# A diffusion transformer block on one core: finer first loads, Q stepped over its rows, and modulation work moved to later stages

## Chip, cores, metric

The kernel runs on one core of one Trainium2 chip. The time is device time in microseconds (us) of one execution. Times of runs made in one session share that session's executions of the kernel before, and where I compare kernels of two sessions I compare their ratios to it.

## The reference, cut to what matters

B = 2 sequences of N = 256 tokens, D = 1152 features, H = 2 heads, F = 4608; everything in bf16.

```python
mod = (_silu(c) @ w_mod).reshape(B, 6, 1, D)
shift_a, scale_a, gate_a, shift_m, scale_m, gate_m = [mod[:, i] for i in range(6)]
h = _layernorm(x, axis=-1) * (1 + scale_a) + shift_a
qkv = (h @ wqkv).reshape(B, N, 3, H, Dh)
...                                          # softmax(q k^T) v, per head
a = ... @ wo
x = x + gate_a * a
h2 = _layernorm(x, axis=-1) * (1 + scale_m) + shift_m
m = _gelu(h2 @ w_fc1) @ w_fc2
return x + gate_m * m
```

So the stages on TensorE are: scale vector and K (which can start with scale_a alone; the shift is added later), Q, scores, V, attention times V, w_o, the first MLP matrix, the second. About 48 MB of weights are read once, roughly in that order. LN2 below is the second layer norm, that of h2; a "hole" is a stretch in which TensorE stands idle.

## The kernel before: the parts that matter

The token tiles are t = 0..3 (two per batch), the feature blocks k = 0..8. All loads go out in order on one queue.

```python
for b in range(B):                                   # x in two loads
    nc.sync.dma_start(x_sb[:, b * TPB:(b + 1) * TPB, :], x_v[:, b, :, :])
KGROUPS = [(0, 2), (2, 4), (4, 6), (6, 9)]           # scale columns and K rows, in turn
for k0, k1 in KGROUPS:
    nc.sync.dma_start(w_scale_a[:, :, k0 * P:k1 * P], ...)
    nc.sync.dma_start(w_k[:, k0:k1, 0:KM1 * P], ...)
nc.sync.dma_start(w_k[:, :, KM1 * P:D], ...)
w_shift_a = load_rows("w_shift_a", ...)
w_q = load_panels("w_q", wqkv_v, 0)                  # three column panels
w_gate_a, w_v, w_shift_m, w_scale_m, w_o, w_f1[0], w_f1[1] = ...   # load_rows each
...
warm(2, pwarm)                                       # matmuls on zeros, 512 columns
nc.tensor.transpose(pc[:], c_sb[:], ident[0:B * KD, 0:B * KD])
...
warm(14, pwarm)
act_stats()                                          # tile 1 on ScalarE, others on VectorE
for j in range(NPD):
    stats_piece(0, j)
...                                                  # tile by tile: norm, transpose, modulate, K
for m in range(KD):                                  # Q, one 128-column block at a time
    for k in range(KD): ...matmul(pacc, w_q[:, k, m * P:(m + 1) * P], hT[:, k, :])
    evac(qT[:, m, :], pacc[:], attn_scale)
    if m == 6:
        gate_a = gate_natural(0, w_gate_a)           # matmuls, then out to DRAM and back, broadcast
```

The w_o stage is pipelined in program order: the statistics of a group are emitted after the multiply of the next one. LN2's normalised rows go through a DMA transpose that ScalarE issues.

```python
BETWEEN = {2: ((0, "d"), (1, "d"), (2, "a"), (3, "a")), 3: ((8, "d"),)}
...
for o, (t, i) in enumerate(order):
    last = o == len(order) - 1
    if last:
        ln2_modulate(0, 4)
    wo_group(t, i, i < NPD - 1)                      # 9 matmuls, times gate_a, plus x
    if o:
        ln2_stats(*order[o - 1])                     # after a tile's third: sqrt, BETWEEN[t], norm,
    if last:                                         # and nc.scalar.dma_start_transpose
        ln2_modulate(0, 5, "a")                      # "a": on ScalarE
        ln2_modulate(0, 7, "a")
        ln2_modulate(0, 6)
```

Of the kernel before, what the change touches and what calls it, by code (L numbers as in the profile page):

```python
# [19 lines left out]
def kernel(  # L20
# [64 lines left out]
    for b in range(B):  # L85
        nc.sync.dma_start(x_sb[:, b * TPB:(b + 1) * TPB, :], x_v[:, b, :, :])
# [11 lines left out]
    KGROUPS = [(0, 2), (2, 4), (4, 6), (6, 9)]  # L98
# [3 lines left out]
    for k0, k1 in KGROUPS:  # L102
        nc.sync.dma_start(
            w_scale_a[:, :, k0 * P:k1 * P],
            wmod_v[:, :, S_SCALE_A * D + k0 * P:S_SCALE_A * D + k1 * P],
        )
        nc.sync.dma_start(w_k[:, k0:k1, 0:KM1 * P], wqkv_v[:, k0:k1, D:D + KM1 * P])
    nc.sync.dma_start(w_k[:, :, KM1 * P:D], wqkv_v[:, :, D + KM1 * P:2 * D])
# [10 lines left out]
    def load_panels(name, view, col0):  # L119
        w = wide_tile(name)  # L120
        for n in range(NPD):
            nc.sync.dma_start(w[:, :, n * PW:(n + 1) * PW], view[:, :, col0 + n * PW:col0 + (n + 1) * PW])
        return w

    w_shift_a = load_rows("w_shift_a", wmod_v, S_SHIFT_A * D)
    w_q = load_panels("w_q", wqkv_v, 0)
    w_gate_a = load_rows("w_gate_a", wmod_v, S_GATE_A * D)
    w_v = load_rows("w_v", wqkv_v, 2 * D)
    w_shift_m = load_rows("w_shift_m", wmod_v, S_SHIFT_M * D)
    w_scale_m = load_rows("w_scale_m", wmod_v, S_SCALE_M * D)  # L130
    w_o = load_rows("w_o", wo_v, 0)
    w_f1 = [None] * 4
    w_f1[0] = load_rows("w_f1_0", wfc1_v, 0)
    w_f1[1] = load_rows("w_f1_1", wfc1_v, D)
# [23 lines left out]
    warm(2, pwarm)  # L158
# [9 lines left out]
    nb1 = small.tile([P, NT], FP32, name="nb1", tag="nb1", bufs=1)  # L168
# [9 lines left out]
    T_ACT = 1  # L178
# [5 lines left out]
    def act_stats():  # L184
        for f, dst in ((ACT.Identity, dsum), (ACT.Square, dsq)):
            nc.scalar.activation(
                xns[T_ACT][:], x_sb[:, T_ACT, :], f, bias=pivot, scale=-1.0, accum_out=dst[:],
            )
# [15 lines left out]
    def recip1(t, with_nb=False):  # L204
        nc.vector.reciprocal(rstd1[:, t:t + 1], rstd1[:, t:t + 1])
        if with_nb:
            nc.vector.scalar_tensor_tensor(
                nb1[:, t:t + 1], mv1[:, t, 0:1], -1.0, rstd1[:, t:t + 1], op0=ALU.mult, op1=ALU.mult
            )

    def norm1(t, c0, c1, eng):
        if eng == "a":
            nc.scalar.activation(
                xns[t][:, c0:c1], x_sb[:, t, c0:c1], ACT.Identity,
                bias=nb1[:, t:t + 1], scale=rstd1[:, t:t + 1],
            )
        else:
            nc.vector.tensor_scalar(
                xns[t][:, c0:c1], x_sb[:, t, c0:c1], mv1[:, t, 0:1], rstd1[:, t:t + 1],
                op0=ALU.subtract, op1=ALU.mult,  # L220
            )
# [4 lines left out]
    def scale_group(g):  # L226
        k0, k1 = KGROUPS[g]
        pm = aux_tile([P, k1 - k0, B], "pm")
        for j in range(k0, k1):
            for k in range(KD):  # L230
                nc.tensor.matmul(
                    pm[:, j - k0, :], w_scale_a[:, k, j * P:(j + 1) * P], sT[:, k, 0:B],
                    start=(k == 0), stop=(k == KD - 1),
                )
        return lambda: nc.vector.tensor_scalar_add(scale_a[:, k0:k1, :], pm[:], 1.0)
# [8 lines left out]
    def modulate(pt, i, k, t0, j0, w, eng):  # L244
        b = t0 // TPB
        dst, src, sc = hT0[:, k, t0 * P:t0 * P + w], pt[:, i, j0:j0 + w], scale_a[:, k, b:b + 1]
        if eng == "d":
            nc.vector.tensor_scalar_mul(dst, src, sc)
        else:
            nc.scalar.mul(dst, src, sc)  # L250

    def modulated_transpose(k):
        pt = transpose_x([k], range(NT))
        for b in range(B):
            modulate(pt, 0, k, b * TPB, b * N, N, "da"[k % 2])
# [41 lines left out]
    CUT = 4 * P  # L297
    warm(14, pwarm)
    act_stats()
    for j in range(NPD):  # L300
        stats_piece(0, j)
    stats_piece(2, 0)
    stats_piece(2, 1)
    add0 = scale_group(0)
    sqrt1(0)
    act_stats_finish()
    recip1(0, True)
    sqrt1(T_ACT)
    norm1(0, 0, CUT, "d")
    add0()  # L310
    pt_0 = transpose_x([0, 1], [0])
    recip1(1)
    modulate(pt_0, 0, 0, 0, 0, P, "a")
    modulate(pt_0, 1, 1, 0, 0, P, "a")
    norm1(1, 0, CUT, "d")
    warm(2, pwarm)
    pt_1 = transpose_x([0, 1], [1])
    modulate(pt_1, 0, 0, 1, 0, P, "a")
    modulate(pt_1, 1, 1, 1, 0, P, "a")
    k_step(0, 0, P)  # L320
    k_step(1, 0, P)
    stats_piece(2, 2)
    sqrt1(2)
    for j in range(NPD):
        stats_piece(3, j)
    k_step(0, P, N)
    norm1(0, CUT, D, "a")
    sqrt1(3)
    recip1(2)
    warm(1, aux_tile([P, T], "pwarm2"))  # L330
    pt_2 = transpose_x([2, 3], [0, 1])
    scale_group(1)()
    k_step(1, P, N)
    modulate(pt_2, 0, 2, 0, 0, N, "a")
    modulate(pt_2, 1, 3, 0, 0, N, "a")
    norm1(2, 0, CUT, "d")
    recip1(3)
    norm1(3, 0, CUT, "d")
    k_step(2, 0, N)
    for ks, e in (((0, 1), "d"), ((2, 3), "a")):  # L340
        pt_3 = transpose_x(ks, [2, 3])
        for i, k in enumerate(ks):
            modulate(pt_3, i, k, 2, 0, N, e)
    k_step(3, 0, N)
    norm1(1, CUT, D, "d")
    norm1(2, CUT, D, "d")
    norm1(3, CUT, D, "d")
    k_step(0, N, T)
    scale_group(2)()
    k_step(1, N, T)  # L350
    modulated_transpose(4)
    k_step(2, N, T)
    modulated_transpose(5)
    k_step(3, N, T)
    k_step(4)
    scale_group(3)()
    modulated_transpose(6)
    k_step(5)
    modulated_transpose(7)
    k_step(6)  # L360
    modulated_transpose(8)
# [8 lines left out]
    def vec_section(stat, w, name):  # L370
        pn = aux_tile([P, CTW], "pn")
        for k in range(KD):
            wk4 = w[:, k, :].rearrange("p (j q r) -> p q j r", q=4, r=32)
            for i in range(4):
                nc.tensor.matmul(  # L375
                    pn[32 * i:32 * i + SW, :].rearrange("p (j r) -> p j r", r=32),
                    stat[:, k, :], wk4[:, i, :, :],
                    start=(k == 0), stop=(k == KD - 1), tile_position=(0, 32 * i),
                )
        dst = act.tile([P, KD, 32], FP32, name=name)  # L380
        nc.vector.transpose(dst[:].rearrange("p k c -> p (k c)"), pn[:])
        return dst
# [5 lines left out]
    shift_a = vec_section(sT, w_shift_a, "shift_a")  # L388
    k_panel(8)

    hT = act.tile([P, KD, T], BF16, name="hT")
    for k in range(KD):
        for b in range(B):
            dst, src = hT[:, k, b * N:(b + 1) * N], hT0[:, k, b * N:(b + 1) * N]
            if (k * B + b) % 3 < 2:
                nc.vector.tensor_scalar_add(dst, src, shift_a[:, k, b:b + 1])
            else:
                nc.scalar.activation(dst, src, ACT.Identity, bias=shift_a[:, k, b:b + 1])
# [69 lines left out]
    gate_a = None  # L468
    for m in range(KD):
        pacc = acc_tile([P, T], "pacc")  # L470
        for k in range(KD):
            nc.tensor.matmul(  # L472
                pacc[:], w_q[:, k, m * P:(m + 1) * P], hT[:, k, :],
                start=(k == 0), stop=(k == KD - 1),
            )
        evac(qT[:, m, :], pacc[:], attn_scale)
        if m == 6:
            gate_a = gate_natural(0, w_gate_a)



# [11 lines left out]
    def attn_transpose(i):  # L493
        pair = attn_all[:, TPB * i:TPB * (i + 1), :].rearrange("p i n -> p (i n)")
        nc.scalar.dma_start_transpose(attnT_all[:, i, :].rearrange("p (c n) -> p c n", n=P), pair)
# [21 lines left out]
    def softmax(b, h):  # L517
# [10 lines left out]
        def finish():  # L528
# [6 lines left out]
            attn_transpose(i)  # L535
# [15 lines left out]
    for i, (pnl, t) in enumerate(v_order):  # L551
        if i < len(softmaxes):
            softmaxes[i]()
        v_group(pnl, t)
        if i == 9:
            shift_m = vec_section(sT, w_shift_m, "shift_m")
            scale_m = vec_section(sT, w_scale_m, "scale_m")
            nc.vector.tensor_scalar_add(scale_m[:, :, 0:B], scale_m[:, :, 0:B], 1.0)

    w_f1[2] = load_rows("w_f1_2", wfc1_v, 2 * D)  # L560
# [8 lines left out]
    def av_tile(chunks, b):  # L569
        pa = acc_tile([P, len(chunks), N], "pa")  # L570
        for ci, cc in enumerate(chunks):
            for kc in range(TPB):
                vt = v_sb[:, b * TPB + kc, cc * P:(cc + 1) * P]
                dst = pa[:, ci, :].rearrange("p (q n) -> p q n", n=P)
                for h in (range(H) if cc == HC else [cc // HC]):
                    rows = half(h) if cc == HC else slice(0, P)
                    av = nc.tensor.matmul(  # L577
# [4 lines left out]
        return av  # L582

    for b in range(B):
        for chunks in ((0, 1), (2, 3), (5, 6), (7, 8)):
            av = av_tile(chunks, b)
            if b == 0 and chunks[0] == 0:
                tc.add_manual_dep(first_load["w_f1_0"], av.ins.name, WAIT_FOR, reason="transposes first")
# [63 lines left out]
    for o, (t, i) in enumerate(order):  # L652
# [3 lines left out]
        wo_group(t, i, i < NPD - 1)  # L656
        if o:
            ln2_stats(*order[o - 1])
# [33 lines left out]
    for b in range(B):  # L692
# [13 lines left out]
        if b == 0:  # L706
            mods = [ln2_modulate(1, k) for k in range(KD)]
            tc.add_manual_dep(first_load["w_f1_2"], mods[0].ins.name, WAIT_FOR, reason="transposes first")
# [84 lines left out]
```

## Time and profile before

| | before |
|---|---|
| time, median | 245.31 us (245.11 to 245.61) |
| TensorE busy | 237.0 of 244.1 us |
| mean granted clock | 1.000 |
| first scale matmul / first K matmul | 9.13 / 10.70 us |
| first MLP matmul / last matmul begins | 98.76 / 240.07 us |

From the page of the kernel before: the span, TensorE's busy time (busy us, share, instructions), the granted clock in 40 slices in tenths, and the first line of the chain that ended last, by engine.

```profile
span 244.1 us, 3930 instructions
...
PE 237.0 (97%) x1679; PEld 142.6 (58%) x1679; DVE 91.7 (38%) x198; ACT 62.1 (25%) x122; POOL 25.4 (10%) x37
...
PEclk9999999999999999999999999999999999999999
...
PE 89%; DVE 4%; DMA 2%; ACT 2%; ACTq 1%; issue 1%; DVEq 0%
```

TensorE is all that counts. It is busy for almost the whole span, so an edit can only win time in which it waits or runs slowly. The granted clock of the page has its first record at 8.96 us here, when the clock went to full; the digits before it read 9 because nothing is on record there, and the spacing of the matmuls shows the half speed instead (warm-ups 0.427 us apart, 0.216 us later). The step to full is called the switch below.

The timeline of TensorE at the start (start us, length us, engine, line, operation, out<-in, shapes, count; in brackets the idle time before and who ended it):

```profile
3.35 5.95 PE L156 MATMUL pwarm<-zeros 128*128 128x512 bf16 x14
9.13 0.59 PE L231 MATMUL pm<-sT,w_scale_a 128*128 128x2 bf16 x18
...
9.70 0.59 PE L156 MATMUL pwarm<-zeros 128*128 128x512 bf16 x2
...
10.70 1.17 PE L263 MATMUL pk<-big,w_k 128*128 128x128 bf16 x18
...
13.53 0.82 PE L263 MATMUL pk<-big,w_k 128*128 128x256 bf16 x6 [0.44 <-ACT big L250]
```

Read it so: 14 warm-up matmuls of 512 columns take 5.95 us, 0.427 us each, twice what such a matmul takes later (0.216 us start to start). They last until the first scale weights are there (landed at 8.72 us in the trace). K then begins in pieces of 128 columns, and there are waits for normalised rows.

The same view at the first MLP matrix:

```profile
81.20 17.72 PE L632 MATMUL pacc<-w_o,big 128*128 128x384 bf16 x108
98.76 3.44 PE L682 MATMUL pacc<-hT,w_f 128*128 128x256 bf16 x30
102.55 65.14 PE L682 MATMUL pacc<-hT,w_f 128*128 128x256 bf16 x393 [0.36 <-ACT hT L600]
```

```profile
99.17 1.35 ACT L622 ACTIVATE xn<-x,nb,rstd 128x1152 bf16<-128x1152 f32 x1
100.55 1.30 ACTq L623 DMA_TRANSPOSE hT<-xn  x1
101.90 1.09 ACT L600 ACTIVATE hT<-hT,shift_m,scale_m 128x256 bf16<-128x256 bf16 x2 [1.38 <-issue]
```

After 30 matmuls TensorE stops for 0.36 us by the view; measured start to start (from one matmul's start to the next one's, less the usual spacing) it is 0.52 us. It waits for a modulation on ScalarE (line L600).

### The profile page before, as it was taken

How to read it: one execution, taken by the hardware profiler on the slowest of the kernel's cores; microseconds unless marked ns; L12 is line 12 of the kernel's file. 1: busy time of each engine (PE TensorE's matmuls, PEld its weight loads, DVE VectorE, ACT ScalarE, POOL GpSimd, SP SyncE). 2: the span in 40 equal slices, each digit the busy share in tenths (PEclk: the TensorE clock that was granted, in tenths of full speed). 3: DMA queues.
4: the chain of work that ended last, by engine and by line, in shares of the span. 5: the costliest groups of instructions: out<-in, count | busy, mean ns of one | idle time of the engine just before them, and what ended most of it. 6: DMA issues, size and time to landing. Idle time of an engine off the chain costs nothing.

```text
span 244.1 us, 3930 instructions
## 1 busy us (share of the span) xinstructions
PE 237.0 (97%) x1679; PEld 142.6 (58%) x1679; DVE 91.7 (38%) x198; ACT 62.1 (25%) x122; POOL 25.4 (10%) x37
## 2 busy tenths in 40 slices
PE   6999999999999999999999999999999999999993
PEld 2585444456667665788854444444665656565673
DVE  2761562126414589913006999910000000000001
ACT  6632251145122521671422233322000000000000
POOL 1000000031000233200000000001222111111111
PEclk9999999999999999999999999999999999999999
DMA  6999999999996999227999994799300000010000
GB/s 227 327 333 360 371 326 390 391 390 393 342 374 93 385 392 182 48 51 249 393 392 374 326 327 121 221 327 320 102 16 16 19 16 16 17 33 19 16 19 16
DMA packets 47308, 53.28 MB, mean 218 GB/s; under 512 B 8371, under 2 KB 34107, under 8 KB 47291
## 3 DMA queue, kind: packets, MB, share of 16 engines
q1 hardware_dynamic: 39840, 50.14, 61.0%
q10 hardware_dynamic: 6939, 1.71, 5.1%
q0 software_dynamic: 512, 1.19, 1.4%
q8 instruction: 13, 0.21, 0.4%
q14 instruction: 4, 0.03, 0.0%
HBM read 50.14 MB, written 1.19 MB: 210 GB/s over the span
## 4 chain that ended last, share of the span: by engine, by line
PE 89%; DVE 4%; DMA 2%; ACT 2%; ACTq 1%; issue 1%; DVEq 0%
PE pacc L738 29%; PE pacc L682 28%; PE pacc L543 7%; PE pacc L472 7%; PE pk L263 4%; PE pk L292 2%; PE pwarm L156 2%; PE pacc L632 2%; PE pa L577 2%; PE ps_s L501 2%; PE pn L375 1%; DMA hT<-xn 1%; DVE stats L646 1%; DMA c_sb<-in_c_dram 1%; DVE tmp L637 1%; ACT xn L622 1%
## 5 line engine op out<-in xcount | busy, mean ns | idle before, releaser
L682 PE MATMUL pacc<-hT,w_f 128*128 128x256 bf16 (+1 forms) x432 | 70.7, 326 | 0.4 <-ACT hT L600 0.4
L738 PE MATMUL pacc<-w_f,gT 128*128 128x384 bf16 (+2 forms) x468 | 70.5, 314 | 0.0
L738 PEld LDWEIGHTS <-gT 128*128 128x128 bf16 x468 | 44.4, 98 | 26.2
L682 PEld LDWEIGHTS <-w_f 128*128 128x128 bf16 x432 | 42.2, 98 | 28.2 <-issue 0.5
L744 DVE TENSOR_TENSOR tmp<-pacc,gate 128x384 f32<-128x384 f32 (+2 forms) x13 | 6.8, 526 | 65.6 <-PE pacc L738 57.8
L714 ACT ACTIVATE gT<-pacc 128x512 bf16<-128x512 f32 x24 | 14.3, 597 | 32.7 <-PE pacc L682 32.7
L424 DVE SCALAR_TENSOR_TENSOR part<-w_gate_m,s,part 128x1152 f32<-128x1152 bf16 x16 | 21.3, 1413 | 0.0
L543 PE MATMUL pacc<-w_v,hT 128*128 128x384 bf16 x108 | 17.9, 326 | 0.0
L472 PE MATMUL pacc<-hT,w_q 128*128 128x512 bf16 x81 | 17.8, 379 | 0.0
L632 PE MATMUL pacc<-w_o,big 128*128 128x384 bf16 x108 | 17.7, 326 | 0.0
L746 POOL TENSOR_TENSOR o_sb<-tmp,x 128x384 bf16<-128x384 f32 (+1 forms) x12 | 11.6, 970 | 54.4 <-DVE tmp L744 54.4
L632 PEld LDWEIGHTS <-big 128*128 128x128 bf16 x108 | 10.5, 98 | 7.0 <-issue 0.2
L543 PEld LDWEIGHTS <-hT 128*128 128x128 bf16 x108 | 10.4, 98 | 7.2 <-issue 0.4
L263 PE MATMUL pk<-big,w_k 128*128 128x256 bf16 (+2 forms) x90 | 13.4, 294 | 0.4 <-ACT big L250 0.4
L472 PEld LDWEIGHTS <-w_q 128*128 128x128 bf16 x81 | 7.8, 98 | 9.9 <-DMA w_q<-in_wqkv_dram 0.5
L638 POOL TENSOR_TENSOR x<-tmp,x_sb 128x384 f32<-128x384 f32 x8 | 7.3, 912 | 35.3 <-DVE tmp L637 35.3
L263 PEld LDWEIGHTS <-w_k 128*128 128x128 bf16 x90 | 7.5, 98 | 3.4 <-issue 0.4
L156 PE MATMUL pwarm<-zeros 128*128 128x512 bf16 x19 | 8.0, 580 | 1.2 <-DVE eps_t L93 1.2
L703 ACT ACTIVATE gT<-pacc 128x512 bf16<-128x512 f32 x12 | 6.5, 598 | 9.5 <-PE pacc L682 9.5
L422 DVE TENSOR_SCALAR part<-w_gate_m,s 128x1152 f32<-128x1152 bf16 x2 | 1.6, 818 | 17.6 <-DMA w_gate_m<-in_w_mod_dram 17.6
L446 POOL DMA_DIRECT2D gates_dram<-nat_v x2 | 1.1, 531 | 68.0 <-DVE nat_v L444 68.0
L637 DVE TENSOR_TENSOR tmp<-pacc,gate 128x384 f32<-128x384 f32 x12 | 6.6, 547 | 2.7 <-PE pacc L632 2.7
(93 smaller groups left out, 156.4 us busy)
## 6 DMA issues: line engine op xcount, KB each, us to landing
w_f<-in_w_fc_dram SPq DMA_DIRECT2D x14, 864.0 KB, 10.2
w_f<-in_w_fc_dram SPq DMA_DIRECT2D x2, 2592.0 KB, 15.5
w_f<-in_w_fc_dram SPq DMA_DIRECT2D x2, 1728.0 KB, 10.5
w_shift_a<-in_w_mod_dram SPq DMA_DIRECT2D x3, 864.0 KB, 11.4
w_q<-in_wqkv_dram SPq DMA_DIRECT2D x3, 864.0 KB, 12.0
w_gate_a<-in_w_mod_dram SPq DMA_DIRECT2D x3, 864.0 KB, 10.0
w_v<-in_wqkv_dram SPq DMA_DIRECT2D x3, 864.0 KB, 13.3
w_shift_m<-in_w_mod_dram SPq DMA_DIRECT2D x3, 864.0 KB, 15.2
```

What stands on the lines that cost most here:

```text
L156: nc.tensor.matmul(dst[:], zeros[:, 0:P], zeros[:], start=True, stop=True)
L263: nc.tensor.matmul(pk[m][:, c0:c1], w_k[:, k, m * P:(m + 1) * P], hT0[:, k, c0:c1], start=(k == 0 and c0 == 0), stop=(k == KD - 1), skip_g ...
L424: nc.vector.scalar_tensor_tensor(part[:, b, :], wg[:, k, :], s32[:, k, b:b + 1], part[:, b, :], op0=ALU.mult, op1=ALU.add,)
L472: nc.tensor.matmul(pacc[:], w_q[:, k, m * P:(m + 1) * P], hT[:, k, :], start=(k == 0), stop=(k == KD - 1),)
L543: nc.tensor.matmul(pacc[:], hT[:, k, t * P:(t + 1) * P], w_v[:, k, pnl * PW:(pnl + 1) * PW], start=(k == 0), stop=(k == KD - 1),)
L632: nc.tensor.matmul(pacc[:], aT[:, k, t * P:(t + 1) * P], w_o[:, k, c0:c1], start=(k == 0), stop=(k == KD - 1),)
L637: nc.vector.tensor_tensor(tmp[:], pacc[:], gate_a[:, b, c0:c1], op=ALU.mult)
L638: (nc.gpsimd if pool_add else nc.vector).tensor_tensor(x1[:, t, c0:c1], tmp[:], x_sb[:, t, c0:c1], op=ALU.add)
L682: nc.tensor.matmul(dst, w_f1[m // KD][:, k, ml * P:(ml + 1) * P], hT[:, k, c0:c1], start=start, stop=(k == KD - 1), **kw,)
L714: nc.scalar.activation(gT[:, m, :], pacc[:], ACT.Gelu_apprx_tanh)
L738: nc.tensor.matmul(pacc[:], gT[:, kk, t * P:(t + 1) * P], w_f2[j][:, r, c0 - n * PW:c0 - n * PW + cw], start=(kk == 0), stop=(kk == KF - 1),)
L746: (nc.vector if last else nc.gpsimd).tensor_tensor(o_sb[:], tmp[:], x1[:, t, c0:c0 + cw], op=ALU.add)
```

## The change

The intent, as far as the diff tells: let the first token tile arrive alone and start its statistics sooner, take the first matmuls in whole batches, keep loads just ahead of use (w_shift_a in two column groups between the rows of Q, Q stepped over k), bring w_o forward, and hold the modulation and MLP loads until the attention transposes are done. Three single warm-up matmuls that the kernel before has in the holes of the front (at 9.70, 9.91 and 11.70 us in its trace) are gone. The core of the diff, with cuts:

```diff
-    for b in range(B):
-        nc.sync.dma_start(x_sb[:, b * TPB:(b + 1) * TPB, :], x_v[:, b, :, :])
+    for t in range(TPB):
+        nc.sync.dma_start(x_sb[:, t, :], x_v[:, 0, t, :])
+    nc.sync.dma_start(x_sb[:, TPB:2 * TPB, :], x_v[:, 1, :, :])
...
-    KGROUPS = [(0, 2), (2, 4), (4, 6), (6, 9)]
+    SGROUPS = [(0, 2), (2, 4), (4, 6), (6, 8), (8, 9)]
...
-    w_q = load_panels("w_q", wqkv_v, 0)
+    SHG = [(0, 5), (5, 9)]
+    QROWS = [[(0, 3), (3, 5)], [(5, 7), (7, 9)]]
+    for (j0, j1), rows in zip(SHG, QROWS):           # shift columns, then rows of Q
...
+    w_v = load_rows("w_v", wqkv_v, 2 * D)
     w_gate_a = load_rows("w_gate_a", wmod_v, S_GATE_A * D)
-    w_v = load_rows("w_v", wqkv_v, 2 * D)
-    w_shift_m = ...
-    w_scale_m = ...
     w_o = load_rows("w_o", wo_v, 0)
...
-    warm(2, pwarm)
+    warm(4, pwarm)
...
-    warm(14, pwarm)
+    warm(13, pwarm)
...                                                  # statistics: tile 2 on ScalarE
+    norm1(0, 0, CUT, nc.vector)                      # CUT: 256 columns
+    norm1(0, CUT, D, nc.gpsimd)                      # the other 896 on GpSimd; the same for tile 1
...                                                  # K in steps of 256 columns
+    vec_section(sT, w_shift_a, shift_a, *SHG[0])
+    shift_chunks(*SHG[0])
...
+    for k in range(KD):                              # Q stepped over k, six accumulators
+        for m in range(KM1):
+            q_mm(m, k)
+        if k == 3:
+            vec_section(sT, w_shift_a, shift_a, *SHG[1])
+            shift_chunks(*SHG[1])
...                                                  # in V:
-        if i == 9:
-            shift_m = ...; scale_m = ...
+        if i == 7:
+            gate_a = gate_natural(0, w_gate_a)
...
+    tc.add_manual_dep(first_load["w_shift_m"], transposed.ins.name, WAIT_FOR, ...)
...                                                  # in w_o:
+        if o == 2:
+            vec_section(sT, w_shift_m, shift_m)
+        if o == 5:
+            vec_section(sT, w_scale_m, scale_m)
```

## The prediction

> **What bounds it now.** TensorE. The page gives PE 237.0 of 244.1 us (97%); the chain of waits is PE for 89%. From 13.5 us on the matmuls stand back to back (timeline: 128x512 every 0.216 us). Only time in which PE waits or warms up can be won. Timeline and chain show: 9.13 us before the first scale matmul (after warm-up matmuls; its weights landed at 8.72); then to 13.5 us about 1.7 us: three warm-up matmuls (0.64), waits for the normalised rows of token tile 1 (0.46) and for modulation on ACT (0.60); 0.15 at 19.9 us (last scale group, landed 20.19); 0.2 at 33.9 us (first Q panel, landed 34.08); 0.52 at 102 us (first MLP matmuls wait for LN2). Winnable after 9.13 us: about 2.6 us, 1%.
>
> **What the change does, costed.**
> 1. Token tile 0 lands alone: the first half of x landed at 4.83 us, so its statistics start about 0.7 us sooner. But scale group 0 has the same bytes ahead of it and still lands near 8.7, and 13 cold warm-up matmuls of 0.427 us still end near 8.9. [...] Four early warm-ups may bring the switch forward. Gain 0.2 to 0.4 us.
> 2. The chain statistics, sqrt, reciprocal, norm is re-cut. With the durations of before (statistics piece 0.47, aggregate 0.24, sqrt 0.29, norm 0.35 to 0.5) I schedule: scale group 0 at 8.95, K from 10.2 (before 10.7); idle 0.6 before it, 0.7 before the transposes of batch 1 (norms of tiles 2 and 3 done at 12.2), 0.7 before its second transposes (896-column norms, done at 15.2). Holes 2.0 us against 1.7: the front gives back what point 1 wins.
> 3. Scale groups of two blocks and Q by rows: the waits at 19.9 and 33.9 us vanish: -0.35.
> 4. shift_a in two sections. One section of 36 matmuls takes 1.29 us: four column groups side by side, 0.122 us for 288 columns, plus 0.1 at each change over. Two with 160 and 128 columns: estimated +0.2 to +0.6 us.
> 5. Q stepped over k in six accumulators: same matmuls, no new wait (evictions of 0.6 to 0.7 us on two engines fit).
> 6. gate_a in V and the modulation sections in the w_o stage: the same PE time, moved. The attention transposes run without competing loads (before, 9 to 14 us to landing), but PE did not wait for them. Token tiles 0 and 1 finish about 1.4 us sooner and the sections (2.3 us) cover LN2: -0.5 us at 102 us. gate_a lands near 82 us; six accumulators absorb it.
>
> **Net** about -0.5 us. Predicted 244.9 us, range 243.4 to 246.4. Faster by over 2%: 2%; within 2%: 95%; slower by over 2%: 3%.
>
> **What would show it.** Scale matmuls from 8.7 to 9.0 us, K at 10.2; PE idle 1.5 to 2.2 us in all between 9 and 16 us; no PE wait on the last scale group or on Q; two shift_a sections at 1.5 to 1.9 us together; attention transposes landing in about 4 us; no PE idle in the first MLP matmuls; PE end 0.3 to 1 us sooner.
>
> **What would make it wrong.** The clock warming much later or sooner; GpSimd's norm holding up VectorE; [...] gate_a so late that LN2 slips and the MLP waits; the held loads arriving late for the modulation sections or the MLP.

Two passages are cut from this text: in point 1 the reason that I gave for a switch that comes sooner, and one of the risks. With the middles of the ranges, -0.3 (point 1), +0.3 (the holes of point 2), -0.35, +0.4 and -0.5 us make -0.45, which I wrote as about -0.5. That four early warm-ups may bring the switch forward, and the 0.2 to 0.4 us for it, were my estimate: the trace of before shows the spacing of the warm-ups go from 0.427 to about 0.215 us at 8.9 us, and not what sets that moment. The norms of 0.35 to 0.5 us in point 2 are an estimate too: before has norms of 512 and 640 columns on VectorE, of 0.41 and 0.44 us, and the line through these gives 0.35 us for 256 columns and 0.50 for 896.

## The result

The changed kernel takes 249.34 us (248.86 to 249.64, 4 runs) against 245.31 us: ratio 1.0161, 95% interval 1.0144 to 1.0179. It is slower by 4.0 us, where I had expected it to be 0.4 us faster, and it lies outside my range. A ratio here is the mean time of one kernel's runs over that of the other's of the same rounds, so it is not quite the ratio of the medians.

The same lines of the page, after:

```profile
span 247.5 us, 3960 instructions
...
PE 237.6 (96%) x1685; PEld 142.7 (58%) x1695; DVE 92.7 (37%) x199; ACT 61.1 (25%) x118; POOL 32.2 (13%) x39
...
PEclk9959999999999999999999999999999999999999
...
PE 79%; DMA 9%; DVE 5%; ACT 2%; issue 1%; POOL 1%; ACTq 1%; SPq 0%; DVEq 0%; POOLq 0%
```

TensorE's busy time hardly moved, but the third of the forty slices shows a clock of 0.5, and only 79% of the chain is TensorE. The mean clock of the four executions was 0.985, 0.985, 0.986 and 0.992; none of the 40 executions of the kernel before whose clock is listed was under 0.996. The start of TensorE's timeline:

```profile
3.14 3.55 PE L161 MATMUL pwarm<-zeros 128*128 128x512 bf16 x13
9.10 0.60 PE L224 MATMUL pm<-sT,w_scale_a 128*128 128x2 bf16 x18 [2.41 <-DMA w_scale_a<-in_w_mod_dram]
...
10.42 2.04 PE L250 MATMUL pk<-big,w_k 128*128 128x256 bf16 x12 [0.47 <-DVE big L240]
12.93 0.61 PE L234 MATMUL pt<-ident,xn 128*128 128x128 bf16 x4 [0.46 <-DVE xn L211]
...
13.97 1.44 PE L250 MATMUL pk<-big,w_k 128*128 128x256 bf16 x6
...
17.53 1.70 PE L250 MATMUL pk<-big,w_k 128*128 128x256 bf16 x12
```

The thirteen warm-ups now take 3.55 us in place of 5.95. In the trace they are 0.216 us apart from the fourth on, at 4.4 us. They end at 6.5 us and TensorE stands idle until 9.1 us. Then the K matmuls of 256 columns, twelve in 2.04 us, change their spacing at 11.2 us from 0.109 to 0.213 us, and back at 18.0 us. The windows view, 11 to 18 us, before and then after (length, then busy us of each engine, granted clock, DMA share, GB/s):

```profile
11.00:18.00 7.00, 6.56 (x107) 6.01 (x105) 5.08 (x18) 3.37 (x9) 0.00 (x0) 1.00 1.11 332
```

```profile
11.00:18.00 7.00, 6.53 (x54) 4.58 (x52) 3.60 (x14) 1.53 (x4) 1.79 (x1) 0.51 1.16 320
```

In these 7 us TensorE looks as busy as before, 6.53 us, but at half the granted clock (0.51 for 1.00). It ran 54 matmuls in place of 107; since their shapes differ, count the columns that they streamed: about 6900 in place of 12900. In 3.42 us that end 0.1 us before the clock fell, it was busy for 1.50 us, less than half the time (same view of the kernel after):

```profile
7.65:11.07 3.42, 1.50 (x29) 1.31 (x29) 2.48 (x9) 2.48 (x6) 3.42 (x2) 1.00 1.12 342
```

The w_o stage and the first MLP matmuls, after:

```profile
92.53 8.95 PE L642 MATMUL pacc<-w_o,big 128*128 128x384 bf16 x54
102.10 3.43 PE L697 MATMUL pacc<-hT,w_f 128*128 128x256 bf16 x30 [0.62 <-DVE hT L613]
106.10 22.19 PE L697 MATMUL pacc<-hT,w_f 128*128 128x256 bf16 x193 [0.57 <-ACT hT L610]
```

There are 0.62 and 0.57 us of idle time where there was 0.36, and a wait that was not there before is at the head of this stage (list of waits, total us, times, longest):

```profile
DVE tmp L647 <- DMA gate<-gates_dram: 4.9, 1, 4.9
```

In the trace gate_a lands at 86.2 and 87.5 us; w_o's first group was done at 82.6. I had put the landing at 82 us. In the kernel before it landed at 62.7 and 65.2 us.

### The profile page after: what moved, and what is told of

Same layout as the page of the kernel before. It is cut to its first block, busy times and chain, and to the rows that moved or that the text cites. A ratio compares the mean times of both kernels' runs of the same rounds, so it can differ in the third digit from the quotient of the medians.

```text
span 247.5 us, 3960 instructions
## 1 busy us (share of the span) xinstructions
PE 237.6 (96%) x1685; PEld 142.7 (58%) x1695; DVE 92.7 (37%) x199; ACT 61.1 (25%) x118; POOL 32.2 (13%) x39
## 4 chain that ended last, share of the span: by engine, by line
PE 79%; DMA 9%; DVE 5%; ACT 2%; issue 1%; POOL 1%; ACTq 1%; SPq 0%; DVEq 0%; POOLq 0%
PE pacc L753 28%; PE pacc L697 27%; PE pq L473 7%; PE pk L250 5%; PE pacc L550 5%; DMA w_scale_a<-in_w_mod_dram 3%; DMA gate<-gates_dram 3%; PE pk L279 2%; DMA gates_dram<-nat 2%; PE ps_s L508 2%; DMA hT<-xn 1%; DVE tmp L647 1%; PE pt L234 1%; DVE stats L656 1%; ACT xn L632 1%
## 5 line engine op out<-in xcount | busy, mean ns | idle before, releaser
L473 PE MATMUL pq<-hT,w_q 128*128 128x512 bf16 x79 | 17.7, 379 | 0.1
L250 PE MATMUL pk<-big,w_k 128*128 128x256 bf16 (+1 forms) x70 | 15.0, 364 | 0.6 <-DVE big L240 0.5
L464 POOL DMA_DIRECT2D gates_dram<-nat x4 | 2.3, 574 | 59.2 <-DVE nat L461 59.2
```

The source lines that it names most:

```text
L250: nc.tensor.matmul(pk[m][:, c0:c1], w_k[:, k, m * P:(m + 1) * P], hT0[:, k, c0:c1], start=(k == 0 and c0 == 0), stop=(k == KD - 1), skip_g ...
L473: nc.tensor.matmul(pq[m][:], w_q[:, k, m * P:(m + 1) * P], hT[:, k, :], start=(k == 0), stop=(k == KD - 1), skip_group_check=True,)
```

## The experiments

The theory after reading the traces: the loss is the half clock (K) and the late gate (LN2). The rival: the front loses by its own holes (the norms on GpSimd, the order of VectorE's queue), and the sections in w_o load VectorE. All kernels gave correct results.

| run | what it is | median us | ratio to before | 95% |
|---|---|---|---|---|
| after | the change | 249.34 | 1.0161 | 1.0144 to 1.0179 |
| e1_bridge | after, 24 warm-ups for 13 | 248.45 | 1.0130 | 1.0110 to 1.0150 |
| e2_two_early | after, warm-ups 2 and 14 | 247.79 | 1.0101 | 1.0086 to 1.0116 |
| e3_gate_v0 | after, gate_a early in V | 248.12 | 1.0118 | 1.0085 to 1.0151 |
| b1_four_early | before, warm-ups 4 and 13 | 245.30 | 1.0010 | 0.9990 to 1.0030 |
| f0_warm_gate | e2 and e3 together | 247.75 | 1.0103 | 1.0088 to 1.0117 |
| f1_norms_dve | f0, no norms on GpSimd | 246.92 | 1.0074 | 1.0053 to 1.0095 |
| g1_old_front | front of before, rest of after, early gate | 245.96 | 1.0025 | 1.0013 to 1.0037 |
| h1_best | before with the parts that should pay | 245.33 | 1.0006 | 0.9991 to 1.0020 |
| p1_x_split | before, x in three loads | 246.17 | 1.0037 | 1.0014 to 1.0061 |
| p2_f1_x_two | f1, x in two loads | 246.72 | 1.0058 | 1.0046 to 1.0070 |
| g2_gate_late | g1, gate late | 246.26 | 1.0041 | 1.0029 to 1.0053 |
| n1_mod5_early | before, one modulation moved | 244.68 | 0.9976 | 0.9964 to 0.9988 |
| s1_p2_gate_late | p2, gate late | 247.91 | 1.0098 | 1.0085 to 1.0111 |
| s2_p2_four_early | p2, warm-ups 4 and 13 | 246.62 | 1.0046 | 1.0033 to 1.0059 |
| s3_after_x_two | after, x in two loads | 248.05 | 1.0114 | 1.0096 to 1.0133 |

### e1_bridge: warm-ups that last until the weights land

```diff
-    warm(13, pwarm)
+    warm(24, pwarm)
```

> Clock theory (the warm-up matmuls run fast from 4.3 us, end at 6.5, leave TensorE idle for 2.6 us, and the clock is taken back from 11.1 to 17.9 us): 24 instead of 13 warm-ups end near 9 us, the clock stays full, the 256-column matmuls of K are 0.108 us apart throughout, and the time falls by 1.5 to 2.5 us to about 247.2. Rival (the front loses by its holes, the norms on GpSimd and their order, not by the clock): no change, within 0.4 us of 249.3.

Measured 248.45 us; the mean clocks were 0.998, 1.000, 0.993 and 1.000. The clock held in three of the four (what 0.993 means is said in point 1 of the account below), but in the profiled execution the fast spacing came only at 6.9 us, so 24 warm-ups lasted until 10.12 us and the scale matmuls, whose weights were there at 9.74, began 0.4 us late. With the gap filled the clock held in these three, as the clock theory said; its size is missed: 0.9 us in place of 1.5 to 2.5. A fixed number of warm-ups does not fit a switch that came at 4.33 us in the trace of after and at 6.82 us in this one.

### e2_two_early: the warm-ups of before

```diff
-    warm(4, pwarm)
+    warm(2, pwarm)
...
-    warm(13, pwarm)
+    warm(14, pwarm)
```

> The after kernel with the warm-ups of before (2, then 14). If the four early warm-ups brought the switch forward: the switch comes at about 8.9 us again, warm-ups end at 9.1, the clock then holds, and the time is about 247.3. If [...] the four had nothing to do with it: the switch comes at another time, and executions of this kernel differ in mean clock; time anywhere from 247 to 249.5.

Measured 247.79 us, clocks 0.997 to 1.000, the fast spacing from about 8.1 us: nearer the first reading, 0.5 us above its number. But the time of the switch varies as well: in the eleven traces of kernels with warm-ups of 2 and 14 the clock goes to full anywhere from 6.2 to 9.1 us. With full clock the holes of the new front can be read start to start: 0.61 us before K, 1.25 us before the transposes of batch 1, 0.15 and 0.80 us after. I had scheduled 0.6, 0.7 and 0.7.

### e3_gate_v0: the gate's matmuls after the first V group

```diff
-        if i == 7:
+        if i == 0:
             gate_a = gate_natural(0, w_gate_a)
```

> gate_a's matmuls after the first V group instead of the eighth. Gate theory (gate_a landed at 86 to 87 us, 5 us after w_o began, and delays LN2): gate_a lands before 75 us, no idle of TensorE of 0.8 us before the first MLP matmul, time falls by 0.8 to 1.2 us to about 248.3. Rival (the two transposes and the add of the modulation sections fill VectorE): the idle times of 0.8 and 0.7 us stay, within 0.4 us of 249.3.

gate_a landed at 71.1 and 73.3 us. The idle time before the first MLP matmul is gone, and the second hole is 0.43 us start to start, for 0.79 and 0.73 in the kernel after. Its scale matmuls began 0.48 us later than those of the kernel after (9.58 for 9.10 us), so of the 1.1 us that the two holes gave back, 0.54 us is left between the two profiled executions, which both lost the clock. The four executions carry the best evidence on the clock:

```
mean clock   us
0.986        248.71
0.986        249.11
0.997        247.54
0.998        247.33
```

It is one and the same program: 1.5 us between executions that lost the clock and executions that kept it. 1.4% of 247 us is 3.5 us of missing clock: 6.9 us at half speed, as between 11.2 and 18.0 us in the trace of after.

### b1_four_early: only the warm-up counts, on the kernel before

```diff
-    warm(2, pwarm)
+    warm(4, pwarm)
...
-    warm(14, pwarm)
+    warm(13, pwarm)
```

> The before kernel with only the warm-up counts of the change (4, then 13). Clock theory: the switch comes near 4.3 us, the warm-ups end near 6.5, TensorE idles until 8.8; if that alone lowers the clock, K is slowed between 11 and 18 us and the time rises by 1.5 to 2.5 us to about 247.3. If it takes the thinner front of the change as well (holes of 0.6 and 0.8 us) the clock holds and the time is 245.0 to 245.4.

Three executions at 245.21 to 245.34 us with clocks of 0.998 or more; one at 246.27 us with 0.990. So the counts alone can lose the clock on the old front as well; one of four did.

### f0_warm_gate: both undone

The edits of e2 and e3 together, against after:

```diff
-    warm(4, pwarm)
+    warm(2, pwarm)
...
-    warm(13, pwarm)
+    warm(14, pwarm)
...
-        if i == 7:
+        if i == 0:
```

> The after kernel with the warm-ups of before (2, 14) and gate_a's matmuls after the first V group. If the clock (1.5 us, from the run with two early warm-ups) and the late gate (1.2 us, from the run with the early gate, at equal clock) are separate and add up: 249.3 - 1.5 - 1.2 = 246.6, between 246.3 and 246.9. If they hide each other: above 247.2.

A miss: 247.75 us, no better than e2 alone, although the trace shows the MLP holes shrunk as in e3. The profiled execution (247.18 us) began its scale matmuls at 9.53 us against 9.08 in e2. The two profiled executions do differ as their holes say: f0's is 0.78 us shorter than e2's (247.96 us), with 1.15 us less idle at the MLP and scale matmuls that begin 0.45 us later. The others (247.62 to 247.92 us, the slowest at a clock of 0.993) have no trace. On this front the executions of one kernel differ by as much as the effect I wanted to size, so I looked for what makes them scatter.

### f1_norms_dve: f0 without the norms on GpSimd

```diff
-    norm1(0, CUT, D, nc.gpsimd)
...
-    norm1(1, CUT, D, nc.gpsimd)
...
     norm1(2, 0, CUT, nc.vector)
+    norm1(0, CUT, D, nc.vector)
+    norm1(1, CUT, D, nc.vector)
```

> The same, and the two 896-column norms moved from GpSimd (3.4 us each) to VectorE after the first norms of tiles 2 and 3. Lock theory (VectorE's norm waits for GpSimd's to end: 0.8 to 0.9 us in place of 0.35): all norms of 256 columns take 0.35 us, the hole before the transposes of batch 1 falls from 0.9-1.25 to 0.6-0.8 us, time 0.2 to 0.5 us below the run before. Rival (VectorE was not held up, the queue of statistics sets the pace): no change, or slower by the 0.8 us of work that VectorE takes on.

Measured 246.92 us (246.34 to 248.02). First the groups of GpSimd's work in the kernel after (count, busy us, mean ns), and VectorE's timeline there; then the groups of the norms in f1:

```profile
L211 POOL TENSOR_SCALAR xn<-x_sb,mv,rstd 128x896 bf16<-128x896 bf16 x2 | 6.8, 3388 | 4.4 <-DVE rstd L208 4.4
```

```profile
8.65 0.87 DVE L211 TENSOR_SCALAR xn<-x_sb,mv,rstd 128x256 bf16<-128x256 bf16 x1
...
11.66 0.35 DVE L211 TENSOR_SCALAR xn<-x_sb,mv,rstd 128x256 bf16<-128x256 bf16 x1
...
12.12 0.75 DVE L211 TENSOR_SCALAR xn<-x_sb,mv,rstd 128x256 bf16<-128x256 bf16 x1
```

```profile
L211 DVE TENSOR_SCALAR xn<-x_sb,mv,rstd 128x896 bf16<-128x896 bf16 x4 | 1.9, 507 | 0.0
...
L211 DVE TENSOR_SCALAR xn<-x_sb,mv,rstd 128x256 bf16<-128x256 bf16 x4 | 1.4, 346 | 0.1
```

A norm of 896 columns takes 3.39 us on GpSimd and 0.51 us on VectorE. GpSimd's two norms span 6.02 to 9.44 and 9.44 to 12.79 us. Two of VectorE's norms of 256 columns take 0.87 and 0.75 us in place of 0.35, and each ends 0.08 us after one of GpSimd's. These two fit the lock theory, but not every norm inside GpSimd's spans took longer: the one at 11.66 us took 0.35 us inside GpSimd's second, and in s3 below three such norms (at 9.22, 12.14 and 12.59 us) took 0.35 us inside GpSimd's spans, of 7.19 to 10.61 and 10.61 to 13.95 us. In this trace the two longer norms had begun 0.8 and 0.7 us before GpSimd's end, the one of 0.35 us 1.1 us before it (as far as spans on GpSimd can be trusted); what decides it was not tested. The gain in time is less sure. The hole before the transposes of batch 1 fell from 1.21 to 0.80 us, but the next one grew from 0.15 to 0.41 us; it waits for VectorE, which now has the work. See s3 against s1 below.

### g1_old_front: the front of before, everything from the shift loads on of after

Against after, cut to its core (the statistics, norms and K order of before come back as a whole):

```diff
-    for t in range(TPB):
-        nc.sync.dma_start(x_sb[:, t, :], x_v[:, 0, t, :])
-    nc.sync.dma_start(x_sb[:, TPB:2 * TPB, :], x_v[:, 1, :, :])
+    for b in range(B):
+        nc.sync.dma_start(x_sb[:, b * TPB:(b + 1) * TPB, :], x_v[:, b, :, :])
...
-    SGROUPS = [(0, 2), (2, 4), (4, 6), (6, 8), (8, 9)]
+    KGROUPS = [(0, 2), (2, 4), (4, 6), (6, 9)]
...
-    warm(4, pwarm)
+    warm(2, pwarm)
...
-        if i == 7:
+        if i == 0:
```

> The front of the before kernel (x in two loads, warm-ups 2 and 14, scale groups, norms and K order of before) with all of the change from the shift and Q loads on, and the gate after the first V group. If the new front is what is left of the loss (holes 2.9 us against 2.05): 245.6 to 246.0. If the later parts lose (sections split, three more change overs): above 246.3. If the later parts win as I predicted (0.2 at Q, 0.5 at the MLP, against 0.4 lost): 244.9 to 245.3.

Measured 245.96 us, ratio 1.0025: most of what f0 and f1 still lose is in the front, and the later parts together cost 0.6 us. In traces, the sections account for 0.4 of it: two sections for shift_a take 0.83 and 0.71 us of TensorE, 1.54 together, where one took 1.31 with its changes over (+0.23), and each section in w_o interrupts a run of matmuls that the two, side by side in V, interrupted once (+0.2). The hole in the first MLP matmuls, which I had expected to vanish, stayed at 0.50 us.

### h1_best: the parts that should pay, on the kernel before

Five scale groups, Q by rows and stepped over k with shift_a in one section, gate_a left in Q, w_o ahead of the modulation weights, their sections in w_o. Against before, cut:

```diff
-    KGROUPS = [(0, 2), (2, 4), (4, 6), (6, 9)]
+    SGROUPS = [(0, 2), (2, 4), (4, 6), (6, 8), (8, 9)]
...
-    w_q = load_panels("w_q", wqkv_v, 0)
+    for r0, r1 in ((0, 1), (1, 3), (3, 6), (6, 9)):
+        nc.sync.dma_start(w_q[:, r0:r1, :], wqkv_v[:, r0:r1, 0:D])
...
+    for k in range(KD):
+        for m in range(KM1):
+            q_mm(m, k)
...
+        if o == 2:
+            vec_section(sT, w_shift_m, shift_m)
+        if o == 5:
+            vec_section(sT, w_scale_m, scale_m)
```

> The before kernel with only the parts that should pay: scale groups of two blocks, Q loaded by rows and stepped over k (shift_a in one section), gate_a left in Q, w_o loaded before the modulation weights, their sections in the w_o stage, MLP loads held for the transposes. Waits at 19.9, 33.9 and 102 us gone (0.15, 0.2, 0.1 to 0.5), two change overs more (0.2): 244.6 to 245.1, that is 0.2 to 0.7 us below before.

Measured 245.33 us, ratio 1.0006: no gain, and a miss. Two of the waits that I wanted to remove, at 19.9 and 33.9 us, are not in the traces of b1 and n1 either, which have the same loads as before. They belonged to the one execution that was profiled, whose span of 244.1 us is 0.2 us or more above those of the executions run later (243.2 to 243.9). And the hole in the MLP was 0.43 us, wherever the sections stood.

### p1_x_split: only x in three loads

```diff
-    for b in range(B):
-        nc.sync.dma_start(x_sb[:, b * TPB:(b + 1) * TPB, :], x_v[:, b, :, :])
+    for t in range(TPB):
+        nc.sync.dma_start(x_sb[:, t, :], x_v[:, 0, t, :])
+    nc.sync.dma_start(x_sb[:, TPB:2 * TPB, :], x_v[:, 1, :, :])
```

> The before kernel with only x loaded as in the change (two single token tiles, then batch 1). If the finer loads themselves make what follows land later (scale group 0 landed at 9.0 to 9.7 us in six traces of the new front, at 8.7 to 9.0 in four of the old): scale group 0 lands at 9.1 to 9.7, the first scale matmul starts that much later, time 0.2 to 0.6 us above before. Rival (the lateness comes with the rest of the new front, or is chance): lands at 8.7 to 9.0, time within 0.15 us of before.

Measured 246.17 us, 0.9 to 1.0 us above before, more than I had expected, and scattered: 245.36 to 247.43. In its trace batch 1 landed at 7.97 us (before 6.27) and scale group 0 at 9.84 (before 8.72). The bytes are the same. Part of it may be the issue: SyncE issues these loads about 0.45 us apart, so with one load more batch 1 was issued at 1.65 us (before 1.18) and scale group 0 at 2.12 (before 1.65). Even if that shift passes on whole, 1.2 of the 1.7 us by which batch 1 was late, and 0.65 of the 1.1 us of scale group 0, are left without a tested cause. In the traces, batch 1 lands at 5.99 to 6.27 us with two loads, and at 6.87 to 7.97 us with three.

### p2_f1_x_two: the new front with x in two loads

Against f1:

```diff
-    for t in range(TPB):
-        nc.sync.dma_start(x_sb[:, t, :], x_v[:, 0, t, :])
-    nc.sync.dma_start(x_sb[:, TPB:2 * TPB, :], x_v[:, 1, :, :])
+    for b in range(B):
+        nc.sync.dma_start(x_sb[:, b * TPB:(b + 1) * TPB, :], x_v[:, b, :, :])
```

> The run with the norms on VectorE (new front, full clock, early gate: 246.9 us), with x loaded in two halves as before. If the finer loads cost more than the earlier statistics bring: scale group 0 at 8.7 to 9.0 us, time 246.2 to 246.7. If the early statistics are what feeds K: the norms come up to 1 us later, K starts later than 10.5 us, time 247.2 to 247.8.

Measured 246.72 us (246.57 to 246.80). Scale group 0 landed at 9.04. The median is little better than that of f1, but the scatter is gone: 0.2 us in place of 1.7. The first tile landed 0.84 us later than in f1, and K did not start later (10.40 us; f1 10.48). The earlier statistics brought no earlier K. This is the quiet base for the last three runs.

### g2_gate_late: the late gate on the old front

Against g1:

```diff
-        if i == 0:
+        if i == 7:
             gate_a = gate_natural(0, w_gate_a)
```

> The run with the old front (245.96 us), with gate_a's matmuls put back after the eighth V group. On this quieter base the late gate alone should cost 0.9 to 1.3 us: 246.9 to 247.2, with TensorE idle 0.7 to 0.9 us before the first MLP matmul. Rival (the gate matters only behind the slowed front): within 0.3 us of 245.96.

Measured 246.26 us against 245.96: 0.3 to 0.4 us, a miss of my 0.9 to 1.3. Here the gate landed 4.4 us after w_o had begun, in the kernel after 5.1 us. The idle time before the first MLP matmul is absent, and only the second hole grew, from 0.49 to 0.73 us.

### n1_mod5_early: one modulation before the transpose issue

On the kernel before:

```diff
-    BETWEEN = {2: ((0, "d"), (1, "d"), (2, "a"), (3, "a")), 3: ((8, "d"),)}
+    BETWEEN = {2: ((0, "d"), (1, "d"), (2, "a"), (3, "a"), (5, "a")), 3: ((8, "d"),)}
...
-            ln2_modulate(0, 5, "a")
```

> The before kernel with one modulation (chunk 5 of batch 0, on ScalarE) put before tile 2's normalisation and its transpose issue. Order theory (the 0.5 us hole in the first MLP matmuls is ScalarE standing 1.3 us at the issue of tile 2's transpose, not LN2 being late): the hole goes, time 0.3 to 0.6 us below before, 244.7 to 245.0. Rival (LN2's transposes of tiles 0 and 1 land too late): the hole stays or moves to another chunk, within 0.15 us of before.

Measured 244.68 us, ratio 0.9976: it beats both kernels. ScalarE's and TensorE's timelines:

```profile
97.47 1.58 ACT L600 ACTIVATE hT<-hT,shift_m,scale_m 128x256 bf16<-128x256 bf16 x3
98.96 1.33 ACT L622 ACTIVATE xn<-x,nb,rstd 128x1152 bf16<-128x1152 f32 x1
100.32 1.30 ACTq L623 DMA_TRANSPOSE hT<-xn  x1
```

```profile
80.53 17.72 PE L632 MATMUL pacc<-w_o,big 128*128 128x384 bf16 x108
98.09 68.42 PE L681 MATMUL pacc<-hT,w_f 128*128 128x256 bf16 x423
```

The transpose issue still takes 1.30 us, but chunk 5 is modulated before it, and the first MLP matrix runs in one piece of 423 matmuls. So the hole of before was ScalarE's program order. Moving modulation sections, as the change does, could not touch it.

### s1_p2_gate_late: the late gate on the quiet base

Against p2:

```diff
-        if i == 0:
+        if i == 7:
             gate_a = gate_natural(0, w_gate_a)
```

> The quiet base (new front, norms on VectorE, warm-ups 2 and 14, x in two loads, early gate: 246.72 us) with gate_a's matmuls back after the eighth V group. If the late gate costs what the traces show on the new front (holes of 0.8 and 0.7 us against 0.4): 247.5 to 247.9. If it costs what it did on the old front (0.3 us): 246.9 to 247.1.

Measured 247.91 us, ratio 1.0098 against 1.0058: 1.0 us. TensorE around the start of the MLP, p2 and then s1:

```profile
99.72 3.44 PE L696 MATMUL pacc<-hT,w_f 128*128 128x256 bf16 x30
103.42 6.82 PE L696 MATMUL pacc<-hT,w_f 128*128 128x256 bf16 x61 [0.26 <-ACT hT L609]
```

```profile
100.86 3.44 PE L696 MATMUL pacc<-hT,w_f 128*128 128x256 bf16 x30 [0.70 <-DVE hT L612]
104.86 5.40 PE L696 MATMUL pacc<-hT,w_f 128*128 128x256 bf16 x48 [0.57 <-ACT hT L609]
```

### s2_p2_four_early: the early warm-ups on the quiet base

```diff
-    warm(2, pwarm)
+    warm(4, pwarm)
...
-    warm(14, pwarm)
+    warm(13, pwarm)
```

> The quiet base with the warm-ups of the change (4, then 13). Clock theory: in some or all executions the mean clock falls to about 0.986 and these are 1.2 to 1.8 us slower than the base (248.0 to 248.5), while executions at 0.997 or more stay at 246.6 to 247.0. Rival (the clock falls only with the extra idle that the finer x loads leave): all at 0.997 or more, 246.6 to 247.0.

Five executions at 246.48 to 246.83 us with clocks of 0.999 and 1.000. One, the profiled one, at 248.20 us with 0.986: there the warm-ups ran fast from 4.6 us, ended at 6.7, and TensorE idled until 9.1 us. Losing the clock costs 1.6 us on a base that otherwise scatters by 0.4 us, and the idle time of the finer x loads isn't needed for it.

### s3_after_x_two: the kernel after with x in two loads

Against after:

```diff
-    for t in range(TPB):
-        nc.sync.dma_start(x_sb[:, t, :], x_v[:, 0, t, :])
-    nc.sync.dma_start(x_sb[:, TPB:2 * TPB, :], x_v[:, 1, :, :])
+    for b in range(B):
+        nc.sync.dma_start(x_sb[:, b * TPB:(b + 1) * TPB, :], x_v[:, b, :, :])
```

> The after kernel with only x loaded in two halves as before. If the finer loads cost as on the old front (1.0 us): 248.2 to 248.6, with scale group 0 landing at 8.7 to 9.1 us. If the statistics that come 1 us later cancel it: 249.0 to 249.5.

Measured 248.05 us, just under my first range. Scale group 0 landed at 8.61. The executions split by clock: 247.58, 247.91 and 247.97 us at 0.999 or more, 248.12 and 248.51 at 0.992 and 0.991, 249.44 at 0.985. At full clock it equals e2 (247.79) and s1 (247.91), so in the new front the finer loads and the GpSimd norms cost next to nothing as long as the clock holds. What x in two loads won here is mostly that fewer executions lost the clock: three of six, after all four of the kernel after. With so few executions that can be chance.

## Why the prediction was wrong, point by point

Full-clock executions of s3 and e2, at about 247.8 us, p2 at 1.0058 and g1 at 1.0025 give a ladder. All are worked out from the ratios of the table times 245.3 us, the first from medians:

| rung | from, to | us |
|---|---|---|
| the clock taken back | 249.34 to about 247.8 | 1.5 |
| the late gate | s1 1.0098 to p2 1.0058 | 1.0 |
| the new front: statistics and norms re-cut, fillers gone | p2 1.0058 to g1 1.0025 | 0.8 |
| the later parts: sections split and moved, loads, Q, early gate in V | g1 1.0025 to before | 0.6 |
| sum, measured 4.0 | | 3.9 |

The rungs are differences along one path, so that they add up is arithmetic and no test. The first two have one cause each, shown by runs (the first takes s3 and e2 at full clock as equal to s1); the last two are bundles whose parts were not undone one by one. Putting the three filler warm-ups back into the new front was not tried.

1. "Four early warm-ups may bring the switch forward. Gain 0.2 to 0.4 us." **This is the first step that failed, in its sign.** The switch did come forward, from 8.96 us in the trace of before to 4.33 in that of after, but the warm-ups are counted, not timed: there they end at 6.5 us, 2.6 us before the weights land (9.05 us). I had also written that "13 cold warm-up matmuls of 0.427 us still end near 8.9". What ran in place of a gain of 0.2 to 0.4 us was a loss of 1.5. I had named "the clock warming much later or sooner" as a risk, and put no cost on it. With warm-ups of 4 and 13, without the bridge of e1, 11 of 24 timed executions had a mean clock of 0.993 or less; with 2 and 14 it was 3 of 50, all three at 0.993 and in kernels with x in three loads (f0, f1, p1). In a span of 246 us, 0.986 is 6.9 us at half clock, as in the trace of after (6.83 us, from 11.16 to 17.98), and 0.993 is 3.4 us; no trace of an execution at 0.993 was kept, so the 3.4 us are an estimate from clock and span. The loss is shown within single kernels (e3, b1, s2, s3).

   The 17 traces show when it came. In the three that lost the clock, it fell 6.83 us after it had first gone to full, and came back 6.83 us later:

   | traces | first switch, us | clock |
   |---|---|---|
   | after | 4.33 | taken back |
   | s2 | 4.61 | taken back |
   | e3 | 4.91 | taken back |
   | b1 | 5.49 | kept |
   | s3 | 6.44 | kept |
   | e1, 24 warm-ups | 6.82 | kept |
   | 11 traces with 2 and 14 | 6.24 to 9.08 | kept |

   The three with the earliest switch are those in which the clock fell. In the timelines of two of them TensorE idles for 2.41 us (after) and 2.21 us (s2) just before the scale matmuls, where p2, with warm-ups of 2 and 14, has 0.89 us and before none. That this gap costs the clock is supported by e1, where it is filled, and by the counts of executions above; what decides the fall is not shown. Nor is it shown why four early warm-ups bring the switch forward. The traces say only this: with two of them TensorE idles for 1.00 us in before and 0.93 us in p2 ahead of the small matmul that transposes c (at 3.2 us), and after four of them not at all in after; with two the switch came before 6.2 us in no trace, with four between 4.33 and 6.82 us. One and the same kernel both lost and kept the clock (e3, b1, s2, s3), so which executions lose it was not under control.
2. "Scale group 0 has the same bytes ahead of it and still lands near 8.7." Wrong: it landed at 9.05 us in the trace of after, and about 1 us later on the old front (p1), at equal bytes. In both it was issued 0.47 us later, which I had not counted. On the new front this cost scatter more than time. Why finer loads land later was not tested beyond that and stays open.
3. The holes of the front. The first was right (0.6). The second was 1.2 us with norms on GpSimd, where two norms of VectorE took 0.87 and 0.75 us in place of 0.35 (I had named that as a risk but did not cost it), and 0.8 without them. In p2 the holes are 0.64, 0.80, 0.41 and 0.80 us, 2.65 together; in g1, with its warm-ups counted, 1.8. The difference is about the 0.8 us rung. I had said 2.0 against 1.7.
4. "The waits at 19.9 and 33.9 us vanish: -0.35." They were accidents of the one profiled execution and had nothing to give.
5. shift_a in two sections, "+0.2 to +0.6": right, 0.23 us in the trace. Q stepped over k without a new wait: right, apart from one gap of 0.08 us (g1).
6. "gate_a lands near 82 us; six accumulators absorb it." **The second step that failed.** It landed at 86.2 and 87.5 us, and the landing is what I had mis-sized: the read back from DRAM took 6.6 us from issue to landing (79.66 to 86.24; 3.5 us in e3, with the early gate). Why it took so long was not tested. The accumulators did keep TensorE running through w_o, but LN2 follows the gate and used up its slack: 1.0 us (s1). How much slack there was shows in six traces. The first half of the gate landed 4.36 us after the start of w_o in g2, 4.72 in s3, 5.13 in after, 5.20 in e2, 5.22 in s1 and 5.26 in e1; the hole before the first MLP matmul, start to start, was 0, 0.36, 0.79, 0.85, 0.86 and 0.91 us. So in these traces up to about 4.35 us are free, and from there each us of lateness is a us of hole; a second hole grows from between 0.4 and 0.5 to 0.73 us in all six. By this count a gate at 82 us, 0.9 us after the start of w_o, would have been free, as predicted. This also says why g2 cost 0.3 us and s1 1.0: their two holes together grew by 0.24 and 1.17 us.
7. "The sections (2.3 us) cover LN2: -0.5 us." Wrong twice. The hole was ScalarE at a transpose issue (n1), and the sections do not give LN2 a head start, because VectorE took its instructions in program order. From f0, with the gate early, after the sixth group of w_o:

```profile
91.66 0.48 DVE L376 STREAM_TRANSPOSE scale_m<-pn 128x288 f32<-128x288 f32 x1
...
93.21 0.56 DVE L647 TENSOR_TENSOR tmp<-pacc,gate 128x384 f32<-128x384 f32 x1 [0.40 <-PE pacc L642]
93.69 0.55 DVE L656 BATCH_NORM_STATS2 stats<-x 128x6 f32<-128x384 f32 x1
94.27 0.23 DVE L658 BATCH_NORM_AGGREGATE mv<-stats 128x2 f32<-128x18 f32 x1
```

The statistics that complete tile 1 (93.69, then the aggregate) stand behind the multiply of the next group (93.21), and that group's matmuls stand behind the section. So what TensorE does in between should delay LN2 by as much as it delays the end of w_o. This is argued from the order; the hole of g1, which has the sections there, stayed at 0.50 us, which fits.

What stays open: f0's median is no lower than e2's although its trace has 1.15 us less idle at the MLP (and its profiled execution is 0.8 us faster); on the front with x in three loads my runs cannot separate 1 us from scatter. The gain of f1 over f0 (0.8 us in medians) isn't confirmed by s3 against s1.

## What to carry to other kernels

Fill the time to the first weights by something that ends when they land, or check in several executions what the clock does: here a fixed count of warm-up matmuls that started a little earlier ran at double speed (0.216 us apart for 0.427), left a gap of 2.6 us, and cost 1.5 us where I had expected a gain. When work is moved out of the way of TensorE, ask what hangs on its result and how it travels (here a trip through DRAM beside other loads, 6.6 us for the read back), and in which order each engine's queue meets it. Before crediting a change with waits that it removes, look whether they are in more than one execution, and look at the engine that ended the wait: the only gain found here was one instruction put before a 1.3 us DMA issue.
